# A pair's memory products two steps apart from its splits, values split first, and a small cast moved from ScalarE to VectorE

## The chip, the cores and the metric

The kernel runs on one core of one Trainium2 chip. TensorE (PE) does the matrix products, VectorE (DVE), ScalarE (ACT) and GpSimd (POOL) the elementwise work, and the SyncE queue (SP) issues all transfers. The metric is the device time of one execution in microseconds (us), lower is better; the time before is the median of three runs.

## The reference, cut to what matters

Eight batches of 576 tokens. Attention goes through 32 learned memory slots for each of 8 heads, its output through a Fourier mix, a norm and a feed-forward layer:

```python
a   = exp(phi - phi.max(axis=2)); a = a / (a.sum(axis=2) + 1e-9)   # [b,h,s,32]
k_m = einsum('bhsm,bhsd->bhmd', a, k)                               # memory keys
v_m = einsum('bhsm,bhsd->bhmd', a, v)                               # memory values
attn = softmax(q @ k_m.T / 8)                                       # [b,h,s,32]
x = heads_side_by_side(attn @ v_m)
u = x + real(fft(fft(x, axis=1), axis=2))
un = (u - mean(u)) / sqrt(var(u) + 1e-6)
out = u + relu(un @ w_ch1) @ w_ch2
```

## The kernel before, in words

Every float32 operand of a product is split into two float16 words, a high one (the rounded value) and a low one (what is left), and each product is three TensorE products: high by high, low by high, high by low.

The feed-forward layer is the **foreground**: 18 chunks of two token tiles, each with 8 steps `j`. A step is 24 rows of `ph` in TensorE's queue (`ffn1`, 256 columns each) and 12 rows of `po` (`ffn2`, 512 columns each); one step is called a unit here. The attention of the later batches is the **background**: the generator `background()` runs beside the foreground and is advanced a step or so per unit. So in TensorE's queue the short background products stand between the rows of `ph` and `po`. Which instruction stands where in each engine's queue is decided when the program is built, by a scheduler that orders by the place in the code and an instruction's priority; on the chip every queue runs strictly in that order and waits where an operand is late.

For batches 2 to 7 (`b >= NX`) one batch of background is:

1. `pooling_weights`: TensorE turns `phi` (`pf`, `pl`, L388), VectorE takes the maxima, ScalarE the exponentials (L401, L402) and the high words `elt` (L410), VectorE the low words (L411), and a transposing DMA brings them as `et` to token rows (`et<-elt`, twice per batch, for two pairs of heads each).
2. Four pairs of heads `g`, each in `pair_memory`: ScalarE squares values, keys and queries into a dump to get their sizes (L518, L521; the dump is the memory of `kvs`, in which the split words stand), TensorE adds them over the partitions (one row `pm<-scratch,small`, called the **sum row** here), VectorE makes the scales (L275 to L286), then keys and values are split: high words on ScalarE (L532), the keys' low words on VectorE (L539), the values' low words on GpSimd (L535, after a scaled copy by ScalarE, L534). Then come 30 rows `pm` of 64 columns: 15 for the keys and 15 for the values. VectorE reads the result (L560 `kmf`, L561 `vmf`), and the memory keys are split again: high words `km[:, 0]` (L570, on ScalarE), low words (L571, VectorE).
3. `pair_scores` for the pair: queries are split (L587, L588), 18 rows `psc` multiply them by `km`, and the softmax follows (L602 and on).
4. When four pairs are done: `values` (`pv`), `spectrum` (`pa`), `mix_m` and `mix_x` (`pp`, `px`), `add_mix`.

There is one buffer for `kvs`, so the squares of pair `g+1` must wait until the products of pair `g` have read it; there is one buffer for `elt` too.

Of the kernel before, what the change touches and what calls it, by code (L numbers as in the profile page):

```python
# [22 lines left out]
NG = H // 2  # L23
# [18 lines left out]
NX = 2  # L42
# [97 lines left out]
def kernel(  # L140
# [10 lines left out]
    nc = tc.nc  # L151
# [156 lines left out]
    def groups():  # L308

        last = [None]  # L310

        def mm(out, lhsT, rhs, start, stop):
            with tc.issue_after(last[0].ins) if start and last[0] is not None else nullcontext():
                m = nc.tensor.matmul(out, lhsT=lhsT, rhs=rhs, start=start, stop=stop)  # L314
            if stop:
                last[0] = marks["pe"] = m

        return mm
# [190 lines left out]
    def pair_memory(b, g, r, vmf, ivs):  # L509

        n = f"{b}_{g}"
        kv = r[:, :KV].rearrange("p (t w c) -> p t w c", t=NST, w=2)
        q = r[:, KV:]
        if b < NX:
            return q, None, kept_memory(g, vmf), 1.0 / 8.0
        am = tiny("am", 3, 1)
        for w in range(2):
            nc.scalar.activation(  # L518
                kvs[0][:, :, w, :].bitcast(BF16), kv[:, :, w, :], AF.Square, accum_out=am[:, 1 + w : 2 + w]
            )  # L520
        nc.scalar.activation(  # L521
            kvs[1][:, 0:3].rearrange("p t w c -> p (t w c)").bitcast(BF16), q, AF.Square, accum_out=am[:, 0:1]
        )
        pm = psg.tile([P, 512], F32, tag="g", name=f"pm_{n}")
        mm = groups()
        mm(pm[:, 128:131], lhsT=ones, rhs=upper(am), start=True, stop=True)
        sc = tiny("sc", 3, 2)
        isc = tiny("isc", 3, 2)
        norm_scale(sc, isc, pm[:, 128:131], 3, 14, n)
        nc.vector.tensor_copy(out=ivs[:, g : g + 1], in_=isc[:, 2:3])  # L530
        for w in range(2):
            nc.scalar.activation(kvs[0][:, :, w, :], kv[:, :, w, :], AF.Copy, scale=sc[:, 1 + w : 2 + w])  # L532
            if w in KP:
                nc.scalar.activation(kv[:, :, w, :], kv[:, :, w, :], AF.Copy, scale=sc[:, 1 + w : 2 + w])  # L534
                nc.gpsimd.tensor_tensor(  # L535
                    out=kvs[1][:, :, w, :], in0=kv[:, :, w, :], in1=kvs[0][:, :, w, :], op=ALU.subtract
                )
            else:
                nc.vector.scalar_tensor_tensor(  # L539
                    out=kvs[1][:, :, w, :],  # L540
                    in0=kv[:, :, w, :],
                    scalar=sc[:, 1 + w : 2 + w],
                    in1=kvs[0][:, :, w, :],
                    op0=ALU.mult,
                    op1=ALU.subtract,
                )
        for w in range(2):
            i = 0
            for ka, kb in ((0, 0), (1, 0), (0, 1)):
                for t in range(NST):  # L550
                    mm(
                        pm[:, w * 64 : w * 64 + 64],
                        lhsT=kvs[ka][:, t, w, :],
                        rhs=et[:, g // 2, kb, t, 64 * (g % 2) : 64 * (g % 2) + 64],
                        start=(i == 0),
                        stop=(i == 3 * NST - 1),
                    )
                    i += 1
        kmf = tiny("kmf", 64, 2)
        nc.vector.tensor_tensor(out=kmf, in0=pm[:, 0:64], in1=mk[:, 0:64], op=ALU.mult)  # L560
        nc.vector.scalar_tensor_tensor(  # L561
            out=vmf[:, g],
            in0=pm[:, 64:128].unsqueeze(1).to_broadcast([P, 2, 64]),
            scalar=isc[:, 2:3],
            in1=mk[:, 0:64].unsqueeze(1).to_broadcast([P, 2, 64]),
            op0=ALU.mult,
            op1=ALU.mult,
        )
        km = tiny("km", 64).bitcast(F16).rearrange("p (l c) -> p l c", l=2)
        nc.scalar.copy(out=km[:, 0], in_=kmf)  # L570
        nc.vector.tensor_tensor(out=km[:, 1], in0=kmf, in1=km[:, 0], op=ALU.subtract)  # L571
        es = tiny("es", 1, 2)
        nc.vector.tensor_scalar(
            out=es, in0=isc[:, 0:1], scalar1=isc[:, 1:2], scalar2=1.0 / 8.0, op0=ALU.mult, op1=ALU.mult
        )
        return q, sc, km, es
# [568 lines left out]
    def background():  # L1145
# [3 lines left out]
        for b in range(B):  # L1149
# [16 lines left out]
            for step in range(NG + 2) if b > 0 else ():  # L1166
                if step < NG:
                    r = load_pair(b, step)
                if step >= 2:
                    pair_transpose(b, step - 2, ahl.pop(step - 2), attnT)  # L1170
                if 0 <= step - 1 < NG:
                    ahl[step - 1] = pair_scores(b, step - 1, *mem.pop(step - 1), aeo)
                    yield (nt if half_made is None else half_made), 0
                if step < NG:
                    mem[step] = pair_memory(b, step, r, vmf, ivs)
                    yield (nt if half_made is None else half_made), 0
# [244 lines left out]
```

## Time and profile before

| what | value |
|---|---|
| median of 3 runs | 942.03 us (939.44 to 943.83) |
| the profiled execution | 940.64 us, its span 938.9 us |
| TensorE busy | 919.6 us of the span, 98% |
| VectorE, ScalarE, GpSimd busy | 637.2, 500.3, 274.3 us |
| TensorE's granted clock | full speed in all of the span |

A row of a timeline gives the start, the length of a merged group of equal instructions, the engine, the source line, what it writes and reads, the count, and in brackets the idle time before it with what ended it. Matmuls overlap one another, so the pace of a stretch is read from start to start and not from the lengths.

### The profile page before, as it was taken

How to read it: one execution, taken by the hardware profiler on the slowest of the kernel's cores; microseconds unless marked ns; L12 is line 12 of the kernel's file. 1: busy time of each engine (PE TensorE's matmuls, PEld its weight loads, DVE VectorE, ACT ScalarE, POOL GpSimd, SP SyncE). 2: the span in 40 equal slices, each digit the busy share in tenths (PEclk: the TensorE clock that was granted, in tenths of full speed). 3: DMA queues.
4: the chain of work that ended last, by engine and by line, in shares of the span. 5: the costliest groups of instructions: out<-in, count | busy, mean ns of one | idle time of the engine just before them, and what ended most of it. 6: DMA issues, size and time to landing. Idle time of an engine off the chain costs nothing. (4 is left out here: it accounts for less than half of the span.)

```text
span 938.9 us, 20234 instructions
## 1 busy us (share of the span) xinstructions
PE 919.6 (98%) x8180; PEld 698.4 (74%) x8180; DVE 637.2 (68%) x1479; ACT 500.3 (53%) x973; POOL 274.3 (29%) x300
## 2 busy tenths in 40 slices
PE   9999899999999999999999999999999999999998
PEld 8977577676767676777667676757666788888887
DVE  5979967576668666876668666576667665565653
ACT  5658767755375536564557445554555343443331
POOL 1305534242354214571426305240324010101000
PEclk9999999999999999999999999999999999999999
DMA  9958621542365227543464327442546320211001
GB/s 325 385 202 291 159 85 28 120 127 65 110 151 161 64 86 175 136 127 71 104 168 124 90 97 192 104 93 86 124 121 150 97 68 12 58 46 23 24 3 43
DMA packets 125949, 110.19 MB, mean 117 GB/s; under 512 B 101536, under 2 KB 101792, under 8 KB 123808
## 3 DMA queue, kind: packets, MB, share of 16 engines
q1 hardware_dynamic: 125856, 108.90, 41.7%
q8 instruction: 64, 1.05, 0.5%
q14 instruction: 29, 0.24, 0.1%
HBM read 69.16 MB, written 20.45 MB: 95 GB/s over the span
## 5 line engine op out<-in xcount | busy, mean ns | idle before, releaser
L314 PE MATMUL ph<-unring,w1t 128*128 128x256 f16 x3264 | 393.3, 273 | 0.0
L314 PEld LDWEIGHTS <-w1t 128*128 128x128 f16 x3264 | 313.6, 98 | 57.3 <-issue 3.7
L903 PE MATMUL po<-w2s,hring 128*128 128x512 f16 x1152 | 268.0, 379 | 0.0
L903 PEld LDWEIGHTS <-hring 128*128 128x128 f16 x1152 | 111.5, 98 | 111.1
L813 POOL TENSOR_TENSOR scratch<-scratch,small 128x1 f32<-128x1 f32 x36 | 24.7, 688 | 221.1 <-DVE scratch L812 190.2
L894 DVE SCALAR_TENSOR_TENSOR hring<-ph,hring 128x512 f16<-128x512 f32 x96 | 65.4, 682 | 19.2 <-ACT hring L893 18.7
L893 ACT ACTIVATE hring<-ph 128x512 f16<-128x512 f32 x96 | 56.2, 587 | 30.2 <-PE ph L314 30.1
L618 POOL TENSOR_TENSOR aring<-aring,scratch 128x384 f32<-128x384 f32 x28 | 25.6, 913 | 158.8 <-DVE scratch L616 151.2
L314 PEld LDWEIGHTS <-stg 128*128 128x128 f16 x1152 | 43.7, 98 | 15.5 <-issue 5.5
L834 POOL TENSOR_TENSOR ud<-un,ud 128x1024 f16<-128x1024 f32 x17 | 37.1, 2185 | 29.1 <-ACT ud L833 29.1
L612 ACT ACTIVATE aring<-aring,scratch 128x384 f32<-128x384 f32 x24 | 14.7, 611 | 56.7 <-DVE aring L611 56.6
L789 DVE SCALAR_TENSOR_TENSOR uring<-px_t,scratch,share 128x256 f32<-128x256 f32 (+1 forms) x80 | 34.4, 477 | 9.2 <-DMA kept_u<-uring 8.6
L314 PE MATMUL pm<-et,stg 128*128 128x64 f16 (+1 forms) x740 | 31.8, 196 | 7.9 <-DMA et<-elt 5.4
L983 POOL TENSOR_TENSOR uring<-uring,share 128x256 f32<-128x256 f32 x5 | 3.6, 730 | 121.5 <-ACT share L980 121.5
L637 ACT CAST aeo<-eo 128x384 f16<-128x384 f32 x30 | 15.3, 510 | 40.4 <-DVE eo L634 40.2
L602 DVE TENSOR_REDUCE scratch<-psc 128x12 f32<-128x384 f32 x32 | 17.6, 550 | 27.7 <-PE pm L314 22.0
L961 PEld LDWEIGHTS <-hring 128*128 128x128 f16 x315 | 30.8, 98 | 3.6
L807 ACT ACTIVATE un<-uring 128x512 f32<-128x512 f32 x32 | 20.0, 624 | 24.8 <-DMA uring<-kept_u 19.5
L930 DVE TENSOR_TENSOR aring<-aring 128x128 f32<-128x128 f32 x80 | 19.8, 286 | 19.3 <-ACT aring L928 18.6
L626 POOL TENSOR_TENSOR ahring<-aring,ahring 128x320 f16<-128x320 f32 x29 | 25.9, 891 | 23.5 <-ACT ahring L625 23.5
L864 PE MATMUL po<-w2s,hring 128*128 128x512 f32 x64 | 31.0, 607 | 1.4 <-ACT hring L850 1.3
L628 POOL TENSOR_TENSOR aring<-aring 128x128 f32<-128x128 f32 x56 | 30.9, 572 | 2.0
(313 smaller groups left out, 1686.8 us busy)
## 6 DMA issues: line engine op xcount, KB each, us to landing
out<-uring SPq DMA_DIRECT2D x35, 256.0 KB, 2.1
rawt<-in_raw SPq DMA_DIRECT2D x13, 640.0 KB, 4.7
stg<-in_raw SPq DMA_DIRECT2D x13, 640.0 KB, 4.2
stg<-in_w SPq DMA_DIRECT2D x7, 1024.0 KB, 6.4
uring<-kept_u SPq DMA_DIRECT2D x26, 256.0 KB, 2.7
kept_u<-uring SPq DMA_DIRECT2D x23, 256.0 KB, 3.0
rawt<-in_raw SPq DMA_DIRECT2D x15, 384.0 KB, 3.6
stg<-in_raw SPq DMA_DIRECT2D x15, 384.0 KB, 3.1
```

Source lines behind the costliest of these rows:

```text
L314: m = nc.tensor.matmul(out, lhsT=lhsT, rhs=rhs, start=start, stop=stop)
L618: eng.tensor_tensor(out=a, in0=a, in1=sm.unsqueeze(2).to_broadcast([P, 12, M]), op=ALU.mult)
L626: nc.gpsimd.tensor_tensor(out=ahl[:, :, 64:128], in0=av[:, 0:5], in1=ahl[:, :, 0:64], op=ALU.subtract)
L628: eng.tensor_tensor(out=a2[:, i : i + 4], in0=a[:, 0:4], in1=a[:, 4:8], op=op)
L789: nc.vector.scalar_tensor_tensor(out=u[rows, hs], in0=px[rows, hs], scalar=igx[rows], in1=tm[rows, w * NJ + half : w * NJ + half + 256], o ...
L813: nc.gpsimd.tensor_tensor(out=rs, in0=rs, in1=half, op=ALU.pow)
L834: marks[f"ul{c}"] = nc.gpsimd.tensor_tensor(out=ud[:, 1], in0=un, in1=ud[:, 0], op=ALU.subtract)
L864: nc.tensor.matmul(po[t], lhsT=h[:, f, t], rhs=w[:, f], start=(j == 0 and f == 0), stop=(j == NW - 1 and f == UB - 1),)
L893: nc.scalar.activation(h[:, 0], phv, AF.Relu)
L894: nc.vector.scalar_tensor_tensor(out=h[:, 1], in0=phv, scalar=0.0, in1=h[:, 0], op0=ALU.max, op1=ALU.subtract)
L903: nc.tensor.matmul(po[t], lhsT=hs[j][:, lh, f * 2 + t], rhs=w2s[:, j * UB + f, lw, :], start=(j == 0 and f == 0 and i == 0), stop=(j == NW ...
L961: m = nc.tensor.matmul(po[n], lhsT=h[:, la, a], rhs=b[lb], start=(j == 0 and i == 0 and n in ("p1", "p6", "p5", "p4")), stop=(j == NW - 1 ...
```

## The change

`pair_memory` is cut in two: up to the splits it stays where it was, the products and what reads them are a function `pair_products`, called one step of the background later and with a lower priority (150 places back). The values are split before the keys. The high words `km[:, 0]` are cast by VectorE and no longer by ScalarE. From L546 on, the changed file's line numbers stand 5 higher.

```diff
@@ -528,7 +528,7 @@
         norm_scale(sc, isc, pm[:, 128:131], 3, 14, n)
         nc.vector.tensor_copy(out=ivs[:, g : g + 1], in_=isc[:, 2:3])
-        for w in range(2):
+        for w in (1, 0):
             nc.scalar.activation(kvs[0][:, :, w, :], kv[:, :, w, :], AF.Copy, scale=sc[:, 1 + w : 2 + w])
             if w in KP:
...
+        return q, sc, isc, pm
+
+    def pair_products(b, g, vmf, q, sc, isc, pm):
+
+        mm = groups()
         for w in range(2):
             i = 0
             for ka, kb in ((0, 0), (1, 0), (0, 1)):
...
         km = tiny("km", 64).bitcast(F16).rearrange("p (l c) -> p l c", l=2)
-        nc.scalar.copy(out=km[:, 0], in_=kmf)
+        nc.vector.tensor_copy(out=km[:, 0], in_=kmf)
         nc.vector.tensor_tensor(out=km[:, 1], in0=kmf, in1=km[:, 0], op=ALU.subtract)
...
             for step in range(NG + 2) if b > 0 else ():
                 if step < NG:
                     r = load_pair(b, step)
+                if b >= NX and 0 <= step - 1 < NG:
+                    with tc.high_priority(-150):
+                        mem[step - 1] = pair_products(b, step - 1, vmf, *mem.pop(step - 1))
                 if step >= 2:
                     pair_transpose(b, step - 2, ahl.pop(step - 2), attnT)
```

TensorE's queue where pair 0 of batch 4 is multiplied. `pm_0` are the pair's memory products, `ph_0` the foreground of step 0 of a chunk; every product has its weight load ahead of it. Before, all 30 products stand in one piece (the first and the last of them):

```order
L314 LDWEIGHTS w1t
L314 MATMUL ph_0_4469<-unring,w1t 128x256
L314 LDWEIGHTS stg
L314 MATMUL pm_0_4141<-et,stg 128x64
...
L314 MATMUL pm_0_4141<-et,stg 128x64
L314 LDWEIGHTS w1t
L314 MATMUL ph_0_4469<-unring,w1t 128x256
```

Now 14 of them alternate with rows of `ph_0`, and 16 follow in one piece behind them:

```order
L314 MATMUL pm_0_4141<-et,stg 128x64
L314 LDWEIGHTS w1t
L314 MATMUL ph_0_4469<-unring,w1t 128x256
L314 LDWEIGHTS stg
...
L314 MATMUL pm_0_4141<-et,stg 128x64
L314 LDWEIGHTS stg
L314 MATMUL pm_0_4141<-et,stg 128x64
```

Behind the last product of this pair, 5 rows of `ph`, 3 of `po`, 24 of `ph` and 17 of `po` stood ahead of the pair's first `psc`; now 12 rows of `po` and 13 of `ph` do.

ScalarE's queue at the same place, from the norm of a later chunk (L807, L808; L812, L813 in the changed file) to the splits of pair 1 (L532 in both). Before:

```order
L807 ACTIVATE un,scratch<-uring 128x512 x2
L808 ACTIVATE un,scratch<-uring,scratch 128x512
L518 ACTIVATE stg,scratch<-stg 128x5x128
L521 ACTIVATE stg,scratch<-stg 128x768
L518 ACTIVATE stg,scratch<-stg 128x5x128
L808 ACTIVATE un,scratch<-uring,scratch 128x512
L570 CAST scratch<-scratch 128x64
L893 ACTIVATE hring<-ph_0_4469 128x512
L893 ACTIVATE hring<-ph_1_4565 128x512
L833 CAST ud<-un 128x1024
L612 ACTIVATE aring<-aring,scratch 128x384
L532 ACTIVATE stg<-stg,scratch 128x5x128 x2
```

Now:

```order
L813 ACTIVATE un,scratch<-uring,scratch 128x512
L898 ACTIVATE hring<-ph_7_4354 128x512
L813 ACTIVATE un,scratch<-uring,scratch 128x512
L898 ACTIVATE hring<-ph_0_4469 128x512
L518 ACTIVATE stg,scratch<-stg 128x5x128
L838 CAST ud<-un 128x1024
L521 ACTIVATE stg,scratch<-stg 128x768
L518 ACTIVATE stg,scratch<-stg 128x5x128
L898 ACTIVATE hring<-ph_1_4530 128x512
L617 ACTIVATE aring<-aring,scratch 128x384
L532 ACTIVATE stg<-stg,scratch 128x5x128 x2
```

The cast L570 is gone from this queue, and the pair's squares (L518, L521, L518) stand behind the norm and one more eviction of `ph`.

VectorE's queue at the products of pair 1 of batch 4. Before:

```order
L921 TENSOR_TENSOR ud<-un,ud 128x1024
L560 TENSOR_TENSOR scratch<-pm_1_4331,small 128x64
L561 SCALAR_TENSOR_TENSOR vmf<-pm_1_4331,scratch,small 128x128
L571 TENSOR_TENSOR scratch<-scratch 128x64
L894 SCALAR_TENSOR_TENSOR hring<-ph_4_4813,hring 128x512
```

Now:

```order
L644 SCALAR_TENSOR_TENSOR aeo<-aeo,small,eo 128x4x32
L565 TENSOR_TENSOR scratch<-pm_1_4331,small 128x64
L566 SCALAR_TENSOR_TENSOR vmf<-pm_1_4331,scratch,small 128x128
L575 CAST scratch<-scratch 128x64
L576 TENSOR_TENSOR scratch<-scratch 128x64
L899 SCALAR_TENSOR_TENSOR hring<-ph_3_4700,hring 128x512
```

The cast (L575) stands right ahead of the subtraction that needs it, and the pair's four steps follow each other on one engine.

## Rows read from the trace of the kernel before

**Rows 1.** From the page: busy time of the engines in us, share of the span, instructions.

```profile
PE 919.6 (98%) x8180; PEld 698.4 (74%) x8180; DVE 637.2 (68%) x1479; ACT 500.3 (53%) x973; POOL 274.3 (29%) x300
```

**Rows 2.** The waits of TensorE from 165 to 730 us, which is the stretch of batches 2 to 7: who waited for what, us in total, how often, the longest.

```profile
PE pm L314 <- DMA et<-elt: 5.4, 5, 1.8
PE pm L314 <- DVE scratch L812: 1.1, 1, 1.1
PE pm L314 <- DVE stg L539: 1.0, 2, 0.8
PE pm L314 <- POOL stg L535: 0.9, 2, 0.5
PE pm L314 <- ACT stg L532: 0.6, 1, 0.6
PE pv L683 <- DVE share L671: 0.4, 1, 0.4
PE psc L314 <- DVE scratch L571: 0.3, 1, 0.3
```

**Rows 3.** Timeline of TensorE at two places without a wait, to read the pace of its rows; the last line is from the page and gives the weight loads of `pm` and `psc`: count, busy us, mean ns of one.

```profile
250.26 0.82 PE L903 MATMUL po<-w2s,hring 128*128 128x512 f16 x3
250.92 2.78 PE L314 MATMUL ph<-unring,w1t 128*128 128x256 f16 x24
253.54 0.60 PE L388 MATMUL pf<-identf,phs 128*128 128x128 f32 x4
...
268.96 1.04 PE L314 MATMUL pm<-et,stg 128*128 128x64 f16 x30
269.84 0.93 PE L314 MATMUL ph<-unring,w1t 128*128 128x256 f16 x7
...
L314 PEld LDWEIGHTS <-stg 128*128 128x128 f16 x1152 | 43.7, 98 | 15.5 <-issue 5.5 <-DVE stg L539 1.7 <-ACT ud L920 1.7
```

**Rows 4.** Timeline of TensorE at the products of pair 0 of batches 2, 5, 6 and 7 (batch 3 is in rows 3, batch 4 has 1.40 in the same bracket).

```profile
177.05 1.03 PE L314 MATMUL pm<-et,stg 128*128 128x64 f16 x30 [0.39 <-DMA et<-elt]
...
470.75 1.03 PE L314 MATMUL pm<-et,stg 128*128 128x64 f16 x30 [1.18 <-DMA et<-elt]
...
569.18 1.04 PE L314 MATMUL pm<-et,stg 128*128 128x64 f16 x30 [1.77 <-DMA et<-elt]
...
665.02 1.03 PE L314 MATMUL pm<-et,stg 128*128 128x64 f16 x30 [0.71 <-DMA et<-elt]
```

**Rows 5.** Timeline of batch 4 from the turned `phi` to the landed `et`, on TensorE, ScalarE, VectorE and the SyncE queue; the last line is from the groups of instructions, the cast of a chunk's norm over the run (busy us, mean ns).

```profile
353.21 0.60 PE L388 MATMUL pf<-identf,phs 128*128 128x128 f32 x4
...
355.27 0.68 ACT L401 ACTIVATE phs<-pf,scratch 128x512 f32<-128x512 f32 x1
...
359.80 0.78 ACT L410 ACTIVATE elt<-phs,scratch 128x576 f16<-128x576 f32 x1 [0.24 <-DVE scratch L407]
...
362.10 1.27 DVE L411 SCALAR_TENSOR_TENSOR elt<-phs,scratch,elt 128x576 f16<-128x576 f32 x1
...
363.40 1.75 SPq L297 DMA_TRANSPOSE et<-elt  x1
...
367.33 0.78 ACT L410 ACTIVATE elt<-phs,scratch 128x576 f16<-128x576 f32 x1 [0.94 <-DMA et<-elt]
...
L833 ACT CAST ud<-un 128x1024 f16<-128x1024 f32 x17 | 17.7, 1043 | 20.0 <-DVE un L814 20.0
```

**Rows 6.** Timeline of pair 1 of batch 7, from its sum row to its scores and the next pair's sum row.

```profile
671.64 0.17 PE L314 MATMUL pm<-scratch,small 128*128 128x3 bf16 x1
...
674.88 0.88 DVE L539 SCALAR_TENSOR_TENSOR stg<-stg,scratch 128x640 f16<-128x640 f32 x1
...
678.38 1.40 POOL L535 TENSOR_TENSOR stg<-stg 128x640 f16<-128x640 f32 x1
...
682.34 0.45 PE L314 MATMUL pm<-et,stg 128*128 128x64 f16 x10
...
682.84 0.23 DVE L560 TENSOR_TENSOR scratch<-pm,small 128x64 f32<-128x64 f32 x1
...
683.52 0.72 ACT L518 ACTIVATE stg<-rawt 128x640 bf16<-128x640 f32 x1
...
684.50 0.23 DVE L571 TENSOR_TENSOR scratch<-scratch 128x64 f16<-128x64 f32 x1 [1.19 <-ACT scratch L570]
...
687.74 0.70 PE L314 MATMUL psc<-scratch,stg 128*128 128x64 f16 x18
...
688.28 0.17 PE L314 MATMUL pm<-scratch,small 128*128 128x3 bf16 x1
```

**Rows 7.** Timeline of TensorE and VectorE at the last products of pair 3 of batch 5; of VectorE and GpSimd at the splits of pair 3 of batch 6; and then the subtraction L571 over all 24 pairs, with its shortest, middle and longest duration in ns.

```profile
518.08 0.46 PE L314 MATMUL pm<-et,stg 128*128 128x64 f16 x10
...
521.50 1.23 DVE L921 TENSOR_TENSOR ud<-un,ud 128x1024 f16<-128x1024 f32 x1
522.64 0.22 DVE L560 TENSOR_TENSOR scratch<-pm,small 128x64 f32<-128x64 f32 x1
...
612.50 2.12 DVE L539 SCALAR_TENSOR_TENSOR stg<-stg,scratch 128x640 f16<-128x640 f32 x1 [0.21 <-ACT stg L532]
...
611.82 2.13 POOL L834 TENSOR_TENSOR ud<-un,ud 128x1024 f16<-128x1024 f32 x1 [1.81 <-ACT ud L833]
...
L571 DVE TENSOR_TENSOR scratch<-scratch x24: 212/227/2049, 180.7 to 714.0; 128x64 f16<-128x64 f32 x24
```

## Prediction

> **What bounds the kernel now.** I read the page first: TensorE is busy 98% of the span, no other engine above 68% [rows 1]. The change neither adds nor removes a matrix product, so the span is TensorE's fixed work plus the time it stands still. Next I read its waits, over the stretch in which batches 2 to 7 run beside the foreground: 9.7 us in 13 waits, and 11 of the 13 are of `pm` rows [rows 2], the rows that move. Outside the stretch nothing moves: the queues are the same up to batch 2's first pair, and behind batch 7 only foreground is left. This 9.7 us is the ceiling of any gain, by the view's own count. The bracketed idle is counted from the modelled end of the row ahead, and these ends are late: a group of 30 `pm` lasts 1.04 us by its row, but the next group starts after 0.88 [rows 3]. From start to start each of the 13 waits is thus some 0.15 us longer, and the true ceiling about 11.7 us, or 1.2%.
>
> For the pace of TensorE I read rows without a wait, from start to start [rows 3]: 24 rows of `ph` take 2.62 us, 0.109 each; 3 of `po` 0.66, 0.22 each; 30 of `pm` 0.88, 0.029 each. A unit is therefore 24 x 0.109 + 12 x 0.22 = 5.2 us. With these I turn the queue into distances, by counting the rows that stand between two places.
>
> **Part 1: the products of pair 0 and the transposing DMA.** 5.4 of the 9.7 us are pair 0 waiting for `et` [rows 2]. In batch 4 the chain is: `phi` turned at 353.6, exponentials from 355.27, high words at 359.80, low words 362.10 to 363.37, DMA issued at 363.40, landed at 367.33 [rows 5]: 13.7 us. The distance from `phi` to the first product in TensorE's queue was 12.2, hence the wait. Counted in the two queues, the distance changes like this for batches 2 to 7: 16.1, 14.3, 12.2, 14.8, 13.8, 15.1 before and 20.9, 12.9, 15.7, 15.6, 13.2, 13.5 now. So it grows by 4.8, 3.5 and 0.8 in three batches, and shrinks by 1.4, 0.6 and 1.6 in batches 3, 6 and 7: `phi` moves in the queue too, and the products do not everywhere get the unit and a half that the change's words say. If the chain stays as long as it was, the waits left are: batch 2, 0.39 - 4.8, none; batch 3, which had no wait [rows 3], at most 1.4; batch 4 none; batch 5, 1.18 - 0.8 = 0.4; batch 6, 1.77 + 0.6 = 2.4; batch 7, 0.71 + 1.6 = 2.3 [rows 4]. That is 5.1 to 6.5 us: nothing won. But the chain does not stay as long in batches 5 and 6: in ScalarE's queue the norm of a chunk and its cast `ud` stood right ahead of the exponentials there and no longer do, about 2 us each by estimate (the cast alone is 1.04 [rows 5], and a pass of the norm stands beside it). That takes batch 5 to none and batch 6 to about 0.4. I take 2.2 us left (0.4 in batch 6, 1.5 in batch 7, 0.3 in batch 3), with 0.5 and 6.5 as the ends. Gain: 5.4 - 2.2 = 3.2.
>
> The moved step itself issues no transfer; the loads in SP's queue keep their pairs and move with them.
>
> **Part 2: the splits, values first.** From the sum row to the first product the queue had 5.5 us in the middle (pairs 1 to 3), now 6.2; to the last product 10.6, now 10.1. So the key rows start later and the value rows end earlier. In pair 1 of batch 7 the keys' low words were ready at 675.76, 4.1 us behind the sum row at 671.64, and the values' low words at 679.78, 8.1 behind it [rows 6]. Values first puts one cast of ScalarE (L532, about 0.75) ahead of the keys: their low words come at about 4.9, against 6.2 needed. Nothing comes earlier for the values, because the scaled copy that GpSimd needs stays behind the query's cast in ScalarE's queue: 8.1 against about 9.8, where the last ten rows stand. What hides the edit is this slack of 1.3 and 1.7 us; without it, it would cost 0.75 a pair. The waits of this kind before, L539, L535 and L532, sum to 2.5 us [rows 2]. Most of it is one pair, batch 6's last: VectorE's L539 took 2.12 us, against 0.88 elsewhere [rows 6], while GpSimd ran a 2.13 us instruction beside it [rows 7]. In the changed queue that GpSimd instruction no longer stands ahead of this pair's splits. But in six pairs the last ten products now stand only 7.5 to 8.5 us behind the sum row, and 8.1 was the typical readiness. I take 1.2 us left of 2.5; ends 0 and 5 (six pairs by 0.8). Gain: 1.3.
>
> **Part 3: from the products to the scores and to the next pair.** Both distances get shorter: last product to first score 5.0 in the middle before, 3.4 now (shortest 2.8); last product to the next sum row 5.5 before, 4.1 now (shortest 3.3). What has to fit: VectorE reads the result, then casts and subtracts. In pair 1 of batch 7 the last product starts at 682.6, L560 at 682.84, and the low words end at 684.73, of which 1.19 us is waiting for ScalarE's cast, which stood behind the squares [rows 6]. With the cast on VectorE this wait goes. The trace has no such cast on VectorE; it lies between nothing and L571's longest 2.05, and I take L571's middle, 0.23, the same 64 columns [rows 7]. So the high words are ready about 0.8 us and the low words about 1.1 us behind the last product, against 2.8 at least. The squares of the next pair: in the same pair they end at 684.24, 1.6 behind the last product [rows 6], against 3.3 at least. Slack is about 1.7 us in both. It is eaten where VectorE comes late: in pair 3 of batch 5 L921 stood ahead and L560 started 4.3 us behind the last product [rows 7]. Queued behind a late score are the softmax of the pair and all `ph` and `po` rows, so a late score is lost in full. I allow 1.2 us for two such pairs, ends 0 and 17 (24 pairs by 0.7). The waits that go here are the one of `psc` for L571, of `pv`, and one of a sum row: 0.3 + 0.4 + 1.1 = 1.8 [rows 2]. Gain: 1.8 - 1.2 = 0.6.
>
> **Part 4: alternating rows.** 14 products of pair 0 in batch 4, and 56 in all queues together, now stand singly between wide rows. I cost it at nothing: where 30 stand in one piece each takes 0.029 [rows 3], less than one weight load lasts. A weight load takes 98 ns on its own row, so loads overlap what runs [rows 3]. The Trainium skill speaks against this: "TensorE: Matmul & The Clock Gate", section "LDWEIGHTS (loading the stationary operand)", gives a load as its columns over 1.2, 107 ns for 128 columns, and "Back-to-back issue gap" says that the spacing is set by load and product together. By that page a single product between wide rows would cost up to 0.107 us and the 56 of them 6 us; the trace does not bear it out for products in one piece, and for alternating ones no row is shown here.
>
> **The sum.** 3.2 + 1.3 + 0.6 = 5.1 us by the view's count; some 6 fewer waits at 0.15 more each add 0.9, and I round down to 5.5, since new waits may be many and small. The profiled execution took 940.64 us; that gives 935.1. It lies 1.4 below the median of 942.03, on which I forecast: **936.5 us**.
>
> **The rivals.** (a) *Traded waits.* Part 1 keeps its 5.1 to 6.5 us because the DMA lands late whatever stands ahead of the exponentials, and tight pairs lose in part 2 what others win: 8.5 to 10 us of waiting remain, and the time is 940.5 to 943. For it: three of six distances shrink. Against it: ScalarE's queue ahead of two chains is lighter. (b) *Short distances decide, and it is slower.* The next pair's squares must wait for the products, since they are dumped over `kvs`; then L518, L521, L518 take 2.3 us of ScalarE and the sum row stands 3.3 to 5.4 behind. If ScalarE reaches them 1.5 us late, or VectorE the result, each pair costs. For it: L560 was 4.3 late once [rows 7]. Against it: with the same lateness as before only two or three pairs exceed the new distances. It is slower than before from 0.5 us a pair on (24 x 0.5 = 12, against the 9.7 to 11.7 that can be won), and by over 0.5% from 0.7; 0.8 a pair with half the waits won gives 942 + 19 - 6 = 955, 0.6 gives 950. (c) *Weight loads count between wide rows*: if each of the 56 cost one load of 98 ns [rows 3], 5.5 us, the gain is eaten: 942. By that page's rule it would be 942.5. (d) *All waits go*: 942 - 11.7 = 930.3.
>
> **How the numbers follow.** A difference under 0.5%, 4.7 us, cannot be told from no change here (the three runs lie 4.4 apart). Chances: the forecast 50%, its own range 933.5 to 939.5; (a) 28%; (b) 9%; (c) 4%; (d) or close to it 9%. Faster by over 0.5%, below 937.3, are (d) and a little under three quarters of the forecast: 0.46. Slower by over 0.5%, above 946.7, is (b): 0.08. The rest is same: 0.46. For 8 in 10 the range leaves out the bottom of (d) and (b): 931.5 to 943.5.
>
> **What would show it.** Right: TensorE's waits for `et<-elt` fall from 5.4 to about 2, and are left in batches 6 and 7; the idle of VectorE ahead of the subtraction (1.19 us in [rows 6]) is gone; all waits in batches 2 to 7 sum to 4 or 5 us; the background of batch 7 ends some 20 us earlier. Wrong: sum rows (`pm<-scratch,small`) or `psc` rows with idle ahead of them in most pairs (rival b); `et` waits of 5 or more (a); `ph` rows between single products further than 0.14 us apart from start to start (c).

## The result, and the profile after

The changed kernel took **952.72 us** in the median (four runs; 942.93 us for the kernel before beside it): ratio **1.0122 [1.0088, 1.0155]**, slower by 1.2%. In most sets of runs here one or more took 2% longer, or still more, at a lower granted clock: the medians count them in, while the ratios and their 95% intervals leave them out, so kernels are compared by ratio. The forecast was 936.5 us, with a range to 943.5. The profile below is that of a second set of runs of the same kernel (952.92 us); the profiled execution took 953.71 us, its span 951.9.

From the page of the changed kernel, the row that answers to [rows 1]:

```profile
PE 924.7 (97%) x8180; PEld 700.3 (74%) x8180; DVE 649.2 (68%) x1503; ACT 495.8 (52%) x949; POOL 281.9 (30%) x300
```

TensorE still has the same 8180 products. VectorE has 24 instructions more, ScalarE 24 less: the cast. The waits of TensorE in the stretch of batches 2 to 7, from 160 to 745 us, answer to [rows 2] (who waited for what, us in total, how often, the longest):

```profile
PE pm L314 <- POOL stg L535: 3.8, 4, 2.3
PE psc L314 <- DVE scratch L575: 3.6, 2, 2.3
PE pa L707 <- DVE aeo L644: 3.4, 1, 3.4
PE pm L314 <- ACT stg L518: 1.3, 2, 0.9
PE psc L314 <- DVE scratch L576: 1.3, 3, 0.5
PE pm L314 <- ACT stg L532: 1.3, 2, 1.2
PE pm L314 <- DVE stg L539: 0.8, 2, 0.4
PE pm L314 <- DMA et<-elt: 0.7, 2, 0.4
...
```

The wait on which most of the forecast rested is gone: `et<-elt` has 0.7 us left of 5.4. But all waits sum to 17.3 us, where [rows 2] has 9.7. In their place stand waits for split words (L532, L535, L539: 5.9), for the memory keys (`psc`, 4.9), for the next pair's squares (L518, 1.3) and, where nothing waited before, `pa` (3.4).

A second loss is no wait. The stretch as a whole, and two places in it, in the changed kernel (from:to, us, busy us of each engine, granted clock, share of the DMA engines):

```profile
160.00:745.00 585.00, 567.60 (x5224) 401.62 (x5223) 412.91 (x916) 315.24 (x634) 213.11 (x220) 0.99 0.49 118
582.00:592.00 10.00, 8.29 (x62) 5.61 (x63) 8.87 (x18) 6.02 (x11) 5.40 (x6) 0.83 0.35 96
629.00:636.00 7.00, 6.63 (x53) 5.36 (x54) 2.51 (x6) 1.95 (x5) 0.84 (x2) 0.76 0.59 77
```

In the kernel before the same stretch has 1.00. Both dips stand right behind a wait. Counted from start to start with the paces of [rows 3] (0.216 for a row of `po`), waits take 11.8 us of this stretch before and 20.1 now, and rows at half pace add 3.3: together 11.6 of the 13.0 us by which the span grew. So the loss lies where the change acts, in the background of batches 2 to 7.

### The profile page after: what moved, and what is told of

Same layout as the page of the kernel before. It is cut to its first block, busy times and chain, and to the rows that moved or that the text cites. A ratio compares the mean times of both kernels' runs of the same rounds, so it can differ in the third digit from the quotient of the medians.

```text
span 972.3 us, 20239 instructions
## 1 busy us (share of the span) xinstructions
PE 945.8 (97%) x8180; PEld 720.5 (74%) x8180; DVE 648.6 (67%) x1503; ACT 497.1 (51%) x949; POOL 282.4 (29%) x300
## 4 chain that ended last, share of the span: by engine, by line
PE 75%; DVE 10%; DMA 6%; POOL 3%; ACT 3%; issue 2%; SPq 1%; POOLq 0%; ACTq 0%
PE ph L314 29%; PE po L908 18%; PE po L966 9%; PE pm L314 3%; PE po L869 2%; PE pp_t L314 2%; PE ph L852 2%; PE px_t L314 2%; PE psc L314 2%; DMA out<-uring 2%; PE pm L489 2%; PE pa L715 1%; DMA w1t<-in_raw 1%; DMA uring<-kept_u 1%; DVE eo L639 1%
## 5 line engine op out<-in xcount | busy, mean ns | idle before, releaser
L908 PE MATMUL po<-w2s,hring 128*128 128x512 f16 x1152 | 272.4, 380 | 0.0
L623 POOL TENSOR_TENSOR aring<-aring,scratch 128x384 f32<-128x384 f32 x28 | 29.1, 1038 | 137.8 <-DVE scratch L621 112.2
L314 PEld LDWEIGHTS <-stg 128*128 128x128 f16 x1152 | 49.0, 98 | 23.4 <-issue 5.8
L314 PE MATMUL pm<-et,stg 128*128 128x64 f16 (+1 forms) x740 | 40.2, 197 | 6.4 <-POOL stg L535 3.4
L535 POOL TENSOR_TENSOR stg<-rawt,stg 128x640 f16<-128x640 f32 x12 | 21.0, 1751 | 84.4 <-ACT rawt L534 84.0
L794 DVE SCALAR_TENSOR_TENSOR uring<-px_t,scratch,share 128x256 f32<-128x256 f32 (+1 forms) x80 | 34.4, 477 | 5.1 <-DMA kept_u<-uring 2.9
L812 ACT ACTIVATE un<-uring 128x512 f32<-128x512 f32 x32 | 19.9, 623 | 28.4 <-DMA uring<-kept_u 22.2
L780 DVE SCALAR_TENSOR_TENSOR share<-pp_t,scratch,small 128x257 f32<-128x257 f32 (+1 forms) x48 | 21.1, 480 | 17.4 <-ACT small L777 16.6
```

Source lines behind the costliest of these rows:

```text
L623: eng.tensor_tensor(out=a, in0=a, in1=sm.unsqueeze(2).to_broadcast([P, 12, M]), op=ALU.mult)
L794: nc.vector.scalar_tensor_tensor(out=u[rows, hs], in0=px[rows, hs], scalar=igx[rows], in1=tm[rows, w * NJ + half : w * NJ + half + 256], o ...
L908: nc.tensor.matmul(po[t], lhsT=hs[j][:, lh, f * 2 + t], rhs=w2s[:, j * UB + f, lw, :], start=(j == 0 and f == 0 and i == 0), stop=(j == NW ...
```

## The experiments

Theories: **A**, the values standing first carry the loss; **B**, VectorE is held by GpSimd at the new cast; **C**, any other order of the queues moves the time by some microseconds, with no single carrier. From e10 on there is a **D**: keys that are split late cost by themselves, wherever the products stand. The expectations of the first four runs were written before the theories had these letters, and use their own.

**e1, the change itself once more.** No edit; it served for the profile above.

> The changed kernel itself once more, for a profile without the slow start of the first one. Theory 1 (VectorE is held: the small cast, now on VectorE, waits until a long GpSimd instruction has ended, 1.72 us twice in the first profile, and the scores wait for it): waits of psc for the cast of 3 to 4 us again, at the same two pairs. Theory 2 (the distances from products to scores and to the next sum row, 3.4 and 4.1 us in the middle, are too short for ordinary lateness): waits of pm, psc and sum rows spread over many pairs. Theory 3 (the clock): after waits that come close together the granted clock falls to half for some us. Time 951 to 953 by all.

Measured: 952.92 us, ratio 1.0120 [1.0090, 1.0151].

**e2, the cast reads PSUM.**

```diff
-        nc.vector.tensor_copy(out=km[:, 0], in_=kmf)
+        nc.vector.tensor_tensor(out=km[:, 0], in0=pm[:, 0:64], in1=mk[:, 0:64], op=ALU.mult)
```

> The changed kernel, but VectorE makes the memory keys' high words straight from the product in PSUM (times the mask) and not from the SBUF copy kmf; same values, same place in the queue. In the kernel before, the instruction of this form (L560) never took more than 0.226 us. Theory 1: the cast is no longer held, the two waits of 1.5 to 2.5 us at psc go, and what follows them: 946 to 949. Theory 2: nothing changes, 951 to 953.

Measured: 950.91 us, 1.0094 [1.0065, 1.0124]. What it was made for shows in the instruction's durations (shortest/middle/longest, ns), first in e1 and then in e2:

```profile
L575 DVE CAST scratch<-scratch x24: 177/183/1719, 185.7 to 705.2; 128x64 f16<-128x64 f32 x24
```

```profile
L575 DVE TENSOR_TENSOR scratch<-pm,small x24: 206/208/215, 205.3 to 720.5; 128x64 f16<-128x64 f32 x24
```

In e1 the long one looks like this (start, length, engine, line, count, idle before):

```profile
580.93 2.17 POOL L919 TENSOR_TENSOR un<-w2s 128x1024 f32<-128x1024 f16 x1
581.43 1.72 DVE L575 CAST scratch<-scratch 128x64 f16<-128x64 f32 x1
583.18 0.80 DVE L576 TENSOR_TENSOR scratch<-scratch 128x64 f16<-128x64 f32 x1
583.30 0.22 PE L314 MATMUL psc<-scratch,stg 128*128 128x64 f16 x2 [1.33 <-DVE scratch L575]
584.03 0.64 PE L314 MATMUL psc<-scratch,stg 128*128 128x64 f16 x16 [0.41 <-DVE scratch L576]
584.53 4.34 PE L314 MATMUL ph<-unring,w1t 128*128 128x256 f16 x23
```

The cast ends when GpSimd's L919 ends, at 583.1; TensorE waits 1.33 and 0.41 us, and the 23 rows of `ph` behind it take 4.34 us where 24 took 2.78 at full clock [rows 3]. Read from PSUM, none of the 24 is held. By the two ratios that is worth 0.26%, a fifth of the loss, but the two intervals overlap, so not even this much is certain.

**e3, the cast back on ScalarE.**

```diff
-        nc.vector.tensor_copy(out=km[:, 0], in_=kmf)
+        nc.scalar.copy(out=km[:, 0], in_=kmf)
```

> The changed kernel with the high words cast on ScalarE again (products later and values first stay). Theory 1: the hold goes, but the cast stands behind the squares in ScalarE's queue: 944 to 949. Theory 2: as slow as the change or slower, since the chain from products to scores gets longer at a short distance: 952 to 957.

Measured: 953.64 us, 1.0118 [1.0085, 1.0151]. With the cast back on ScalarE the whole loss stays.

**e4, the products later, alone.** The change with keys first and the cast on ScalarE.

```diff
-        for w in (1, 0):
+        for w in range(2):
...
-        nc.vector.tensor_copy(out=km[:, 0], in_=kmf)
+        nc.scalar.copy(out=km[:, 0], in_=kmf)
```

> The kernel before with only the products later (keys first, cast on ScalarE). Theory 1: within 0.5% of the kernel before, 939 to 946. Theory 2: most of the loss is here, 948 to 955.

Measured: 946.50 us, 1.0040 [1.0022, 1.0057]. Up to 740 us its waits are 9.2 us, as in [rows 2], with 4.6 still for `et`; 2.9 us of the excess stand in one place later (`px_t` waits 2.0 us for VectorE's L780, `pp_t` 0.9 for L794). Between e3 and e4 stands one edit, the order of the splits: 0.8%, or 7 us.

**e5, the change with the keys first.**

```diff
-        for w in (1, 0):
+        for w in range(2):
```

> The change with the keys split first again, as before (products later and the cast on VectorE are kept). Theory A, the order of the splits carries the loss: the products later alone gave 946.5 us, with the values first 953.6, so 7 us belong to the values standing first; with the cast on VectorE (952.9 against 953.6, hardly a difference) this kernel lands at 945 to 947.5, and the waits for `stg` (L532, L535, L539) and `pa` fall back to about 4 us. Theory B, VectorE is held by GpSimd at the new cast: the two casts of 1.7 us stay, worth 2 to 2.5 us, and the time is 948.5 to 950. Theory C, any rearrangement of the queues moves the time by some us up or down, without one carrier: nothing can be said but that the parts do not add up, so a time outside 944 to 950.

Measured: 941.15 us, 1.0003 [0.9985, 1.0021]. Below even what A expected, and far from B: with the keys first the whole loss is gone, and no gain is left. Against e4 the cast on VectorE is here worth 0.4%. `et` has 2.7 us and words 1.6, but `psc` now has 3.8, where [rows 2] has 0.3.

**e6, the values first, alone.** The kernel before with the one edit:

```diff
-        for w in range(2):
+        for w in (1, 0):
```

> The kernel before with only the values split ahead of the keys. Theory A: 947 to 949, slower by about 7 us, with waits of TensorE's `pm` rows for key or value words in most batches, since the keys' high words now stand behind the values' in ScalarE's queue and the products are not later. The prediction's part 2 said that the slack hides it: 940 to 942. If the values first hurt only together with later products (through which instructions of GpSimd and VectorE meet), it is 941 to 943 as well, and then A falls as a statement on the edit by itself.

Measured: 950.19 us, **1.0105 [1.0083, 1.0128]**, with a granted clock of 1.00 throughout. TensorE's waits from 160 to 745 us:

```profile
PE pm L314 <- POOL stg L535: 6.6, 6, 2.1
PE pa L702 <- DVE aeo L639: 4.0, 3, 2.0
PE pm L314 <- DVE stg L539: 2.8, 4, 1.0
PE pm L314 <- ACT stg L532: 2.1, 2, 1.1
PE pm L314 <- DMA et<-elt: 1.9, 2, 1.3
PE psc L314 <- DVE scratch L571: 1.1, 1, 1.1
```

Split words: 11.5 us, for 2.5 in [rows 2]; that and `pa`, less 3.5 us won at `et`, are the loss. To see how, pair 2 of batch 6, a quiet one, in the kernel before:

```profile
591.46 0.17 PE L314 MATMUL pm<-scratch,small 128*128 128x3 bf16 x1
593.36 1.53 ACT L532 ACTIVATE stg<-rawt,scratch 128x640 f16<-128x640 f32 x2
594.21 0.89 DVE L539 SCALAR_TENSOR_TENSOR stg<-rawt,scratch,stg 128x640 f16<-128x640 f32 x1
597.01 0.75 PE L314 MATMUL pm<-et,stg 128*128 128x64 f16 x20
597.74 1.42 POOL L535 TENSOR_TENSOR stg<-rawt,stg 128x640 f16<-128x640 f32 x1
```

and the same pair in e6:

```profile
590.86 0.17 PE L314 MATMUL pm<-scratch,small 128*128 128x3 bf16 x1
592.76 1.53 ACT L532 ACTIVATE stg<-rawt,scratch 128x640 f16<-128x640 f32 x2
594.06 0.83 POOL L618 TENSOR_TENSOR aring<-aring,scratch 128x384 f32<-128x384 f32 x1 [8.45 <-DVE scratch L616]
594.33 1.24 DVE L539 SCALAR_TENSOR_TENSOR stg<-rawt,scratch,stg 128x640 f16<-128x640 f32 x1 [0.42 <-ACT stg L532]
595.89 1.23 DVE L588 SCALAR_TENSOR_TENSOR stg<-rawt,scratch,stg 128x768 f16<-128x768 f32 x1
596.40 1.98 POOL L535 TENSOR_TENSOR stg<-rawt,stg 128x640 f16<-128x640 f32 x1
596.75 0.31 PE L314 MATMUL pm<-et,stg 128*128 128x64 f16 x5
597.00 0.60 PE L314 MATMUL pm<-et,stg 128*128 128x64 f16 x15
```

Before, the keys' low words were ready 3.6 us behind the sum row (594.21 + 0.89 - 591.46); now 4.7. The second cast is 0.75 of the 1.1, the rest is L539 itself, 1.24 instead of 0.89 with GpSimd's L618 beside it. The values win almost nothing: L535 starts 5.5 behind the sum row instead of 6.3, but lasts 1.98 instead of 1.42 beside L588, and ends at 7.5 instead of 7.7. No product waits here: the sixth, the first to need the keys' low words, stands at 6.1. Over the 18 pairs 1 to 3 the keys' slack, from ready to needed, has shrunk from 1.8 to 1.3 in the middle. That alone is not the loss.

Pair 1 of batch 7 shows where the loss comes from. In the kernel before its sum row stands at 671.64 [rows 6], and the casts start 2.4 us behind it:

```profile
674.03 1.54 ACT L532 ACTIVATE stg<-stg,scratch 128x640 f16<-128x640 f32 x2
```

In e6 its sum row stands at 667.57:

```profile
668.54 0.63 ACT L807 ACTIVATE un<-uring 128x512 f32<-128x512 f32 x1 [4.03 <-DMA uring<-kept_u]
...
673.81 1.04 ACT L833 CAST ud<-un 128x1024 f16<-128x1024 f32 x1 [2.02 <-DVE un L814]
...
675.28 1.53 ACT L532 ACTIVATE stg<-stg,scratch 128x640 f16<-128x640 f32 x2
676.86 0.32 PE L314 MATMUL pm<-et,stg 128*128 128x64 f16 x5 [1.08 <-ACT stg L532]
677.27 0.81 DVE L539 SCALAR_TENSOR_TENSOR stg<-stg,scratch 128x640 f16<-128x640 f32 x1
678.14 0.61 PE L314 MATMUL pm<-et,stg 128*128 128x64 f16 x15 [0.96 <-DVE stg L539]
680.28 1.39 POOL L535 TENSOR_TENSOR stg<-stg 128x640 f16<-128x640 f32 x1
681.72 0.47 PE L314 MATMUL pm<-et,stg 128*128 128x64 f16 x10 [1.77 <-POOL stg L535]
```

In ScalarE's queue a chunk's norm (L807, L808), which began only when its rows had landed, and its cast L833, which waited 2.0 us for VectorE, stood ahead of the casts, and these started 7.7 us behind the sum row. One late pair makes three waits, 3.8 us. Over the 18 pairs 1 to 3 the casts start more than 4 us behind the sum row once before, and in 6 pairs in e6, each time behind a norm with its cast (L833) or a cast of `ud` that prepares weights (L920). These 6 are among the 7 pairs in which a word came after its place, and most of that lateness is of the values' words, which the exchange by itself makes no later (7.5 against 7.7).

An estimate, pair by pair as in the table further down and with the places kept: of 13.1 us of lateness in e6, 12.6 stay if all keys' low words come 1.1 us earlier, but only 1.1 if no cast starts more than 2.5 us behind its sum row. For the change it is 6.7 and 1.6 of 7.3. So the exchange costs through the other order of ScalarE's queue that comes with it, and hardly through the 1.1 us by which it delays the keys. Why this order puts the norm ahead of the casts more often is not shown.

**e7, the cast on VectorE, alone.**

```diff
-        nc.scalar.copy(out=km[:, 0], in_=kmf)
+        nc.vector.tensor_copy(out=km[:, 0], in_=kmf)
```

> The kernel before with only the small cast of the memory keys on VectorE. By the prediction's part 3 the waits of psc and pv for it go (0.7 us by the view): 940 to 941.5 where the kernel before has 941. Theory B: the cast meets the 2.1 us instruction of GpSimd in one to three of the 24 pairs and lasts until that ends (1.7 us instead of 0.18): 942.5 to 944, with a wait of psc or pv behind it.

Measured: 941.43 us, 1.0005 [0.9987, 1.0022]: nothing. `psc` waits 4.0 us where it had 0.3, `et` 1.3 where it had 5.4.

**e8, another priority.**

```diff
-                    with tc.high_priority(-150):
+                    with tc.high_priority(-100):
```

> The whole change, with the products' priority 100 places back and not 150, so that they stand a little earlier in the queues. Theory A and the prediction's way of counting: the distance from the splits to the products gets shorter by some us and the one behind them longer; waits for stg grow, those of psc shrink: 952 to 956. Theory C: the queues fall out differently and other instructions meet; the time goes to any value between 943 and 957, and the waits of VectorE and GpSimd are at other places than in the change itself.

Measured: 950.34 us, 1.0089 [1.0060, 1.0118]. Words 5.9 us (3.2 of them L535), `psc` 5.3. Below what A expected by 1.7, and no stray value either: with the values first all of e1, e2, e3, e6 and e8 have ratios of 1.0089 to 1.0120, with the keys first e4, e5 and e7 of 1.0040 or less. That speaks against C, a move without a carrier, which so far explains 0.4% at most (e4); e13 below does not keep to this pattern.

**e9, keys and values exchanged throughout.** `KP` says whose low words GpSimd makes.

```diff
-KP = [1]
+KP = [0]
...
-        for w in range(2):
+        for w in (1, 0):
...
-        for w in range(2):
+        for w in (1, 0):
```

> The kernel before with the parts of keys and values exchanged: values split first with their low words on VectorE, keys second with theirs on GpSimd, and the products taken values first. TensorE's queue is the same row by row. Theory A, now sharper: what costs is not that the values are first but that the words which the products need first are ready late against their place in TensorE's queue. Here the first words are again on the first and faster chain: 940 to 942.5, the kernel before. If splitting the values first costs by itself (their layout, the meeting of GpSimd and VectorE), it stays at 947 to 952.

Measured: 940.40 us, 0.9999 [0.9975, 1.0022]. The words are ready and needed as in the kernel before, with keys and values exchanged (table below). So values as such cost nothing in front when the products take them first too. That a split order against the order of need costs by itself does not follow from this run.

**e10, the keys' high words cast twice** (in the kernel before; the second cast writes the same words).

```diff
-            nc.scalar.activation(kvs[0][:, :, w, :], kv[:, :, w, :], AF.Copy, scale=sc[:, 1 + w : 2 + w])
+            for _ in range(2 - w):
+                nc.scalar.activation(kvs[0][:, :, w, :], kv[:, :, w, :], AF.Copy, scale=sc[:, 1 + w : 2 + w])
```

> The kernel before with the keys' high words cast twice, one right behind the other, so that the keys' words are ready some 0.75 us later and ScalarE has 24 casts more (17 us). In TensorE's queue the first product stands about 8.1 us behind the sum row in the middle and no longer 5.5 (counted in the queue); the last one stays at 10.7. Theory A (the slack between ready and needed decides): slack 3.8 where it was 1.6 to 2.1, no waits for key words, 939 to 942. Theory D (the keys being later costs, wherever the products stand, because ScalarE and VectorE come late to what follows): 946 to 950. Theory C (any rearrangement moves the time): outside 938 to 943 with waits elsewhere.

Measured: 939.02 us, 0.9977 [0.9959, 0.9994]. The time came as A expected, but not all of the reason: the second cast fell behind those of the values and the query in ScalarE's queue, and the keys' low words were ready 8.8 us behind the sum row in the middle, not 4.4 to 4.7. The sixth product had moved to 10.0, so 24 casts more and words 4.9 us later cost nothing here, against D.

**e11, the same in e6**, and **e12, the same in the change** (the edit of e10 in both).

> The kernel before with the values split first (950.2 us alone) and the keys' high words cast twice: the keys' words are later still, about 5.5 to 6.1 us behind the sum row in a quiet pair, but the first product stands 9.5 us behind it in the middle of the queue where it stood 6.0; the last one stays at 10.6. Theory A: slack 3.5, the waits for key words go (L532 and L539, 4.9 us by the view in the kernel with the values first alone), a part of those for the values' words stays: 941 to 945. Theory D: 951 to 955.

> The whole change with the keys' high words cast twice: first product 9.0 us behind the sum row in the middle of the queue instead of 6.3, last one 10.6, scores 3.8 behind the last product. Theory A: 942 to 947, most of the loss of the change gone though ScalarE has more to do. Theory D and C: 951 to 957.

Measured: e11 946.38 us, 1.0053 [1.0036, 1.0071], 0.5% below e6 and about 1 us above what A expected. e12 **959.09 us**, 1.0175 [1.0122, 1.0228], where A expected 942 to 947: a clear miss, and above the 951 to 957 of C and D. Its largest wait:

```profile
PE pm L314 <- DVE stg L540: 12.5, 8, 3.5
```

L540 is L539 here. Its words were ready 9.4 us behind the sum row in the middle, the product that needs them stood at 9.9: I had taken 6. So the edit did not give slack to the change, it took nearly all of it.

**e13, e12 with the keys first.**

```diff
-        for w in (1, 0):
+        for w in range(2):
```

> The kernel of the last run (the change with the keys' high words cast twice, 959.1 us) with one edit: keys split first again. In TensorE's queue the sixth product, the first that needs the keys' low words, stands at 9.9 us behind the sum row in both. Theory A, counted as slack: there the keys' low words were ready 9.4 behind the sum row in the middle and 9 of 18 pairs were over; here I expect them at 8.8, as in the kernel before with the double cast (939.0): 940 to 943. Theory D (the double cast itself hurts as soon as the products stand a step later): 952 or more.

Measured: 952.92 us, 1.0126 [1.0106, 1.0147]: A missed again, and the time is what D, now narrowed to later products, expected (952 or more). Its words were ready at 8.6 in the middle, as expected, against 9.9, but six pairs were beyond their place:

```profile
PE pm L314 <- DVE stg L540: 5.3, 3, 4.0
PE pa L708 <- DVE aeo L645: 4.7, 2, 4.5
PE pm L314 <- POOL stg L536: 3.1, 3, 1.7
```

The keys first are thus no guarantee: against e5 the second cast alone costs 1.2%, where in the kernel before it costs nothing (e10). The middle of the slack does not fix the time either.

**e14, e10 once more**, in more runs.

> The kernel before with the keys' high words cast twice, once more, since it came out at 939.02 where the kernel before had 940.91 (ratio 0.9977). If that holds, 939 again, 0.2 to 0.3% below the kernel before; if it was the chip or chance, the ratio is 1.000.

Measured: 938.91 us, 0.9985 [0.9976, 0.9995]. It beats the kernel before by a hair, 0.15%, with 24 casts in it that compute nothing new. So the gain must lie in how its queues fell out, which was not followed further.

**The kernels side by side.** For the 18 pairs 1 to 3 I counted where in TensorE's queue the sixth product (keys' low words) and the sixth product of the values stand behind the sum row, with the same paces as above, and read from each trace when the words were ready (for e9, read keys and values exchanged). "Over" is how many pairs had a word ready after its place, and by how much in sum.

| kernel | first split | ratio | keys' low words: ready / place (middle) | over: pairs, us | waits for words, us |
|---|---|---|---|---|---|
| before | keys | 1 | 3.9 / 5.7 | 3, 3.2 | 2.5 |
| e10 | keys | 0.9977 | 8.8 / 10.0 | 3, 4.3 | 3.8 |
| e9 | as needed | 0.9999 | 3.9 / 5.7 | 3, 4.0 | 3.0 |
| e5 | keys | 1.0003 | 4.4 / 6.2 | 2, 1.9 | 1.6 |
| e7 | keys | 1.0005 | 4.2 / 6.1 | 4, 1.5 | 1.1 |
| e11 | values | 1.0053 | 9.2 / 9.9 | 3, 6.1 | 5.5 |
| e4 | keys | 1.0040 | 4.1 / 5.9 | 5, 4.5 | 3.3 |
| e6 | values | 1.0105 | 5.3 / 6.6 | 7, 13.1 | 11.5 |
| e8 | values | 1.0089 | 5.1 / 6.7 | 7, 8.4 | 5.9 |
| e1 | values | 1.0120 | 5.3 / 6.6 | 8, 7.3 | 5.9 |
| e13 | keys | 1.0126 | 8.6 / 9.9 | 6, 9.7 | 8.4 |
| e3 | values | 1.0118 | 4.9 / 6.6 | 4, 7.9 | 6.8 |
| e12 | values | 1.0175 | 9.4 / 9.9 | 10, 15.5 | 14.1 |

The time follows how much of the words comes after its place, not the middle of the slack: every kernel with 4.5 us or less has a ratio of 1.0040 or less, every one with 7.3 or more of 1.0089 or more. This column was made after the runs, and it does not say why more pairs start late in some of the orders. That stays open.

Five pairs of kernels differ in the order of the splits alone, and in each the values first are slower: e6 and the kernel before (1.0%), e1 and e5 (1.2%), e3 and e4 (0.8%), e11 and e10 (0.8%), e12 and e13 (0.5%, with intervals that overlap). That this edit carries the loss is shown; the way from it to the late pairs is not shown beyond what e6's queues say.

## Why the prediction was wrong, point by point

**What bounds the kernel**: right. TensorE's work did not change, and its waits in batches 2 to 7 with their clock dips make up 11.6 of the 13.0 us.

**Part 1** (a gain of 3.2): right in sign for the kernel as it was built, and too small. `et` fell from 5.4 to 0.7, forecast 2.2. By batches it was right for batch 3 alone (0.27 us, forecast 0.3): the other 0.38 stand in batch 5, where none was forecast, and batches 6 and 7, forecast at 1.9, have none. And it is not the later products that did it: with them alone 4.6 are left (e4), and with the cast alone, which does not move them by a step, 1.3 (e7). Each order of the queues gave another value.

**Part 2** (a gain of 1.3): this is the step that failed. Its words were: "What hides it is this slack of 1.3 and 1.7 us". The slack was well counted in the middle: 1.3 us for the keys, and 5.3 against 6.6 was measured in the change. (The 6.2 in the forecast is the place of the first product, while the low words are first needed by the sixth; this made up for words that came 0.4 later than taken.) What was wrong is that I took the readiness of one quiet pair for all pairs, and so took for granted that in the new queues nothing else would stand ahead of the casts. From it I took 1.2 us of waits, with 5 as the upper end, six pairs by 0.8. Split words cost 5.9 us in the change and 11.5 in e6 alone, because in some pairs the casts start up to 5.8 us later than in a quiet one, most often behind a chunk's norm: in e6 seven pairs were over, by 1.9 each, most of it at the values' words. The forecast also left out who runs beside whom: it named the one L539 of 2.12 us beside GpSimd and put it down as an accident that the new queue removes, but with the values first L539 lasts 1.07 us or more in 11 of the 18 pairs (e1 and e6 alike), where it did in 2. By the estimate under e6 this adds little.

Not in the forecast at all: `pa`, 3.4 us in one wait in e1, 4.0 in three in e6, none in [rows 2]. In e1 it is in batch 6, whose pair 3 was not late: its casts started 1.9 us behind the sum row and no product waited. Its softmax was:

```profile
618.91 0.63 ACT L812 ACTIVATE un<-uring 128x512 f32<-128x512 f32 x1 [4.63 <-DMA uring<-kept_u]
...
620.38 0.60 ACT L617 ACTIVATE aring<-aring,scratch 128x384 f32<-128x384 f32 x1
...
629.37 0.42 PE L707 MATMUL pa<-ct,aeo 128*128 128x290 f16 x1 [3.36 <-DVE aeo L644]
```

The exponentials (L617) could have started at 616.24, when VectorE had their operand ready (L616); they stood behind a norm that waited for its rows, and began 4.1 us later. The wait of 1.8 us in batch 7 of e6 is of the same kind; that of 2.0 in its batch 5 follows a late pair 3. So what the forecast had not priced, at the splits and at `pa`, is the place of the norm in ScalarE's queue.

**Part 3** (a gain of 0.6): wrong in sign. `psc` went from 0.3 to 4.9 us, and sum rows still wait 1.3. The price of the cast in the middle was right (0.183 us measured, 0.23 taken), as was the forecast that ScalarE no longer keeps the subtraction waiting. The rows of L571 before and of L576 now (busy us, mean ns, idle before):

```profile
L571 DVE TENSOR_TENSOR scratch<-scratch 128x64 f16<-128x64 f32 x24 | 8.4, 350 | 18.0 <-ACT scratch L570 17.6
```

```profile
L576 DVE TENSOR_TENSOR scratch<-scratch 128x64 f16<-128x64 f32 x24 | 7.1, 297 | 0.8
```

17.6 us of idle time are gone and nothing was won, since those were not on the path. Lost was the bound that I had written down and then not used for the pairs: 2.05 for the cast. It was 1.72 twice, with a `psc` wait behind it each time.

**Part 4** (alternating rows at nothing): right. Where single `pm` alternate with `po` in e1:

```profile
182.15 0.38 PE L908 MATMUL po<-w2s,hring 128*128 128x512 f16 x1
182.37 0.19 PE L314 MATMUL pm<-et,stg 128*128 128x64 f16 x1
182.40 0.38 PE L908 MATMUL po<-w2s,hring 128*128 128x512 f16 x1
```

From `po` to `po` it is 0.25 us, the 0.22 and 0.029 of [rows 3] added; between two `ph`, 42 times, 0.138, which is 0.109 and 0.029. The Trainium skill's "TensorE: Matmul & The Clock Gate", section "Back-to-back issue gap", read as one load per single product, does not hold for these rows. Rival (c) falls.

**The rivals.** (a), traded waits, was nearest in kind, but it stopped at equal sums. (b) ended on the right side by another road: it looked for the loss behind the products, in most pairs; 5.9 us stood in front of them and 4.9 behind, in a few pairs. **The signs**: batch 7's background ends 8.4 us earlier (its last `px_t` at 733.24 instead of 741.66), not 20. The clock fell after waits, which no step held possible; the 3.3 us of rows at half pace are a quarter of the loss.

In sum, by ratios: the values first cost 0.5 to 1.2% in five pairs of kernels, the cast nothing alone (e7), the later products nothing (e5 against e7) to 0.4% (e4). None of the forecast gain of 5.5 us stood: in e5, without the values' order, what `et` gave back came up again at `psc`.

## What to carry to other kernels

Do not price an exchange of two independent steps by the slack of one quiet repetition. Here the exchange delayed one step by 1.1 us, which fitted into that slack; the loss came with the other order of an engine's queue, and it came in a few repetitions. Before pricing such an exchange at nothing, list ready minus needed for every pair in the new queues, look what now stands ahead of the moved steps and may itself wait (here a norm that waits for its rows), and which instructions of the other engines will newly run beside them. Splitting first what the consumer needs first was the faster order in all five pairs of kernels here, in one of them within the noise. A wait that disappears may come back at the next consumer when all queues run in order, as that of `et` did at `psc` in e5 and e7.

## What the runs showed of the hardware that was not expected

A VectorE instruction of 0.18 us took 1.72 when a GpSimd instruction of 2.17 us ran, and ended with it; the same words read from PSUM took 0.206 to 0.215 in all 24 pairs. The Trainium skill states this in "SBUF — State Buffer", section "Who interferes with whom": VectorE and GpSimd share a pair of ports that one instruction holds until its end. The traces agree, by the cast's two long cases. The milder stretches (L539 from 0.89 to 1.24, L535 from 1.42 to 1.98) go the same way, but are shorter than a hold to the other's end would make them: L539 would have ended at 595.78, 0.89 behind the end of L618, and ended at 595.57. No run separates their share in the loss.

TensorE's granted clock, 1.00 through batches 2 to 7 before, was 0.83 and 0.76 in the windows behind two places where it had stood waiting, with rows at half pace in part of them, the lower of its two levels (1.2 and 2.4 GHz). In e6, with more waiting for words than the change, it stayed at 1.00.
